# Sparse attention and a two-layer MLP on one core: weights loaded ahead of batch 1, each chunk's two layers in turn, one PSUM pool for both

## The chip, the core and the metric

One NeuronCore of one Trainium2 chip. The metric is the device time of one execution in microseconds (us); medians of several executions are given. An execution with a profile also leaves a trace; its "span" runs from the first to the last traced instruction and is about 1.8 us shorter than the time of the same execution (352.0 against 353.79 us for the kernel before).

## The reference

```python
q, k, v: (8, 8, 576, 64)  float32        # batch, heads, sequence, head size
scores = q @ k.T / sqrt(64)
heads 0-3: row sees the last 32 columns;  heads 4-7: row sees every 32nd column (causal)
attn   = softmax(masked scores) @ v
x      = attn as (8*576, 512) = (4608, 512)
h      = x @ w_in                         # (512, 2048)
out    = (max(h, 0) + alpha * min(h, 0)) @ w_out     # (2048, 512)
```

## The kernel before

TensorE (PE in the profile) does all matrix products in float16; here their outputs lie in the PSUM memory, all other tiles in the SBUF. The attention of a batch is cut into "pieces": S (scores), P (value blocks), T (transposes of queries and keys), X (transposes back into `xT`). The 4608 tokens go through the MLP in 9 chunks of 512; a layer of a chunk is 16 pieces of four 512-column matmuls. The pieces of both kinds are laid into each engine's program in the order in which Python calls them.

```python
pspool = tile_pool("ps", bufs=3, PSUM)      # transposes, value blocks
phpool = tile_pool("ph", bufs=2, PSUM)      # first layer
pbpool = tile_pool("pb", bufs=1, PSUM)      # scores, two banks
popool = tile_pool("po", bufs=1, PSUM)      # second layer
# ...
def over_v(b, eng):                          # 32 value rows repeated at other partitions
    v16 = vls[b % 2]
    cast_copy(eng, v16[0:32, 1:24, :], v16[96:128, 0:23, :])
# ... a score piece of a later batch ends on GpSimd:
    nc.scalar.activation(et, sp, Exp, scale=SCALE)
    nc.gpsimd.tensor_tensor(ev, ev, mask, op=mult)
# ... in the list of pieces, stage g (pair g's scores, pair g-1's value blocks):
    def run(...):
        if kind == "P0" and g % 4 == 1:
            over_v(g // 4, "dve")            # right ahead of the first value block
        fn()
        for b, pr in extra:                  # behind it, on GpSimd:
            cast_l(b, pr) ...                # casts of the next batch's q and k, or
            cast_v(b, pr, "pool") ...        # copies of the values
# ... one first-layer piece:
    hps = pspool.tile(...) if alone and m % 3 == 2 else phpool.tile(...)
    4 matmuls -> hps
    nc.scalar.activation(neg, hps, Relu, scale=-1.0)
    late.append(lambda: nc.vector.scalar_tensor_tensor(gT, neg, oma, hps, mult, add))
# ... order of the work behind batch 0 (cut):
for m in range(16): lin1_piece(0, m, True); attn_n(0 if m < 9 else 1, end1)
while pos["i"] < end1: attn_step(end1)       # rest of batch 1, alone
for m in range(16): lin1_piece(1, m, True); attn_n(0 if m < 13 else 1, end2)
for i in range(16): lin2_piece(0, i); attn_n(2 if i % 2 else 1, end2)
# ...
for n in range(2, NCH):                      # batch n+2 runs beside chunk n
    for i in range(16):
        lin2_piece(n, i);     attn_step(ab)
        lin1_piece(n + 1, i); attn_step(ab)
```

The softmax here doesn't subtract the row's maximum and nothing guards it: scores larger than these inputs give would overflow.

## Time and profile before

| | before |
|---|---|
| median time (first 3 runs) | 354.47 us |
| span of the profiled execution | 352.0 us |
| TensorE busy | 96% |
| DVE / ACT / POOL busy | 56% / 50% / 42% |
| granted clock at half | 50.7 to 60.9 us |

DVE is VectorE, ACT ScalarE, POOL GpSimd. The granted clock is what the profile records of TensorE's clock, as a share of full speed. A row of the timeline has the start, the length, engine and line, operation, output and inputs; a bracket has the idle time ahead of it and what ended that.

### The profile page before, as it was taken

What the parts mean: (1) busy time and instruction counts of PE and PEld (TensorE: products, weight loads), DVE (VectorE), ACT (ScalarE), POOL (GpSimd) and SP (SyncE); (2) the same over time, 40 slices, a digit from 0 to 9 for tenths busy, and PEclk for the clock granted to TensorE, in tenths of its full rate; (3) what the DMA queues carried; (4) which work ended last, traced back from release to release, by engine and by line L of the source; (5) the groups of instructions that cost most, each with busy time, mean ns of one, the idle gap of its engine ahead of it and who ended that gap; (6) DMA issues with size and microseconds to landing.
All of it is one profiled execution on the core that took longest, in us unless ns stands there. A gap on an engine that the chain in (4) does not pass through costs nothing.

```text
span 352.0 us, 6757 instructions
## 1 busy us (share of the span) xinstructions
PE 336.4 (96%) x2733; PEld 175.7 (50%) x2733; DVE 198.3 (56%) x391; ACT 176.6 (50%) x313; POOL 147.4 (42%) x164
## 2 busy tenths in 40 slices
PE   7899979999898998999999999999999999999995
PEld 2554544454444544554467665545455444444444
DVE  3487774884443875576557655765575444444400
ACT  2635852665336574656465646565645444444411
POOL 7936726259895583656365532451240000000000
PEclk9999985999999999999999999999999999999999
DMA  7999999934946862553556210000001100100021
GB/s 232 185 203 224 234 253 151 184 34 69 160 99 176 75 164 57 87 48 61 177 85 62 49 47 31 32 31 32 30 32 40 52 30 31 61 30 30 32 89 61
DMA packets 46111, 33.08 MB, mean 94 GB/s; under 512 B 27376, under 2 KB 37760, under 8 KB 46080
## 3 DMA queue, kind: packets, MB, share of 16 engines
q0 software_dynamic: 37312, 16.79, 44.6%
q1 hardware_dynamic: 8768, 15.87, 12.8%
q8 instruction: 21, 0.34, 0.4%
q14 instruction: 10, 0.08, 0.1%
HBM read 36.83 MB, written 9.44 MB: 131 GB/s over the span
## 4 chain that ended last, share of the span: by engine, by line
PE 86%; DVE 4%; POOL 4%; ACT 3%; DMA 1%; issue 1%; SPq 0%; ACTq 0%
PE hps L489 36%; PE ops L534 32%; PE sp L271 3%; PE tp L214 3%; PE pv L318 3%; DVE x L327 2%; PE xp L335 2%; POOL et L305 2%; DMA ql<-in_q_dram 1%; PE wps L556 1%; ACT kT L159 1%; PE sp L287 1%; PE ops L525 1%; ACT osb L539 1%; PE sph L287 1%
## 5 line engine op out<-in xcount | busy, mean ns | idle before, releaser
L502 DVE SCALAR_TENSOR_TENSOR gT<-neg,oma,hps 128x512 f16<-128x512 f32 x144 | 106.9, 743 | 74.7 <-ACT neg L499 72.4
L489 PE MATMUL hps<-xT,win 128*128 128x512 f16 (+1 forms) x640 | 146.7, 361 | 0.1
L534 PE MATMUL ops<-wout,gT 128*128 128x512 f16 x560 | 141.9, 379 | 1.9 <-ACT osb L539 1.6
L499 ACT ACTIVATE neg<-hps 128x512 f32<-128x512 f32 x144 | 86.2, 599 | 95.1 <-PE hps L489 93.6
L305 POOL TENSOR_TENSOR et<-et,consts 128x576 f16<-128x576 f16 (+1 forms) x48 | 61.3, 1277 | 80.5 <-ACT et L295 80.4
L489 PEld LDWEIGHTS <-win 128*128 128x128 f16 x640 | 58.4, 98 | 52.9 <-issue 3.4
L534 PEld LDWEIGHTS <-gT 128*128 128x128 f16 x560 | 49.7, 97 | 50.7 <-issue 2.5
L295 ACT ACTIVATE et<-sp 72x576 f16<-72x576 f32 (+1 forms) x58 | 37.6, 649 | 24.8 <-PE sp L271 11.7
L327 DVE TENSOR_TENSOR x<-pv,rc 72x384 f16<-72x384 f32 (+2 forms) x80 | 42.1, 527 | 2.7
L325 DVE RECIPROCAL rc<-pv 72x6 f32<-72x6 f32 (+2 forms) x80 | 14.9, 187 | 41.7 <-PE pv L318 41.4
L539 ACT COPY osb<-ops 128x512 f32<-128x512 f32 x35 | 20.6, 587 | 27.9 <-PE ops L534 27.9
L318 PEld LDWEIGHTS <-et 72*128 72x128 f16 (+1 forms) x448 | 23.2, 99 | 17.1 <-DVE x L327 1.8
L271 PEld LDWEIGHTS <-kT 64*128 64x128 f16 x448 | 10.9, 95 | 27.8 <-issue 17.7
L271 PE MATMUL sp<-qT,kT 64*128 64x72 f16 (+1 forms) x408 | 17.6, 201 | 3.5 <-ACT kT L159 3.2
L161 DVE COPY qT<-tp 128x1024 f16<-128x1024 f16 (+1 forms) x16 | 17.4, 1085 | 4.1 <-PE tp L214 4.1
L159 ACT COPY kT<-tp 128x1024 f16<-128x1024 f16 (+1 forms) x16 | 14.5, 909 | 6.7 <-PE tp L214 6.7
L556 PE MATMUL wps<-wrm 128*128 128x512 f16 x44 | 16.4, 448 | 1.2 <-DVE wrm L568 1.2
L318 PE MATMUL pv<-vs,et 72*128 72x65 f16 x256 | 15.4, 194 | 2.1 <-POOL et L305 0.8
L335 PEld LDWEIGHTS <-x 72*128 72x128 f16 (+1 forms) x224 | 12.4, 102 | 7.6 <-DVE x L327 2.4
L335 PE MATMUL xp<-consts,x 72*128 72x72 f16 (+1 forms) x224 | 14.7, 208 | 1.0 <-DVE x L327 0.8
L163 POOL COPY vs<-stv 72x1024 f16<-72x1024 f16 x14 | 14.5, 1061 | 0.0
L318 PE MATMUL pv<-vl,et 128*128 128x65 f16 x192 | 12.0, 200 | 1.2 <-DVE vl L161 1.1
(66 smaller groups left out, 189.6 us busy)
## 6 DMA issues: line engine op xcount, KB each, us to landing
out_dram<-osb SPq DMA_DIRECT2D x35, 256.0 KB, 2.0
ql<-in_q_dram SPq DMA_DIRECT2D x6, 512.0 KB, 5.2
kl<-in_k_dram SPq DMA_DIRECT2D x6, 512.0 KB, 5.9
stv<-in_v_dram POOLq DMA_DIRECT2D x8, 288.0 KB, 5.3
vl<-in_v_dram POOLq DMA_DIRECT2D x8, 288.0 KB, 8.3
win<-in_moe_w_in_dram POOLq DMA_DIRECT2D x4, 512.0 KB, 10.3
wout<-in_moe_w_out_dram POOLq DMA_DIRECT2D x4, 512.0 KB, 16.8
qs<-in_q_dram POOLq DMA_DIRECT2D x7, 256.0 KB, 4.6
```

The source lines that it names most:

```text
L271: keep(nc.tensor.matmul(sps[y][:, w * x : w * x + w], P.kT[hf, k0 : k0 + 128], P.qT[hf, w * t : w * t + w], start=(x == 0), stop=(x == len ...
L295: keep(nc.scalar.activation(ev.rearrange("r (y c) -> r y c", y=2), sp[0:r, :, 0:n], AF.Exp, scale=SCALE))
L305: keep(nc.gpsimd.tensor_tensor(ev, ev, m, op=ALU.mult))
L318: keep(nc.tensor.matmul(pv[:, 65 * x : 65 * x + 65], et[0:r, c : c + 128], v16[0:r, 2 * P.pr + hh, t, :] if P.strided else v16[:, 6 * (2 * ...
L327: keep(nc.vector.tensor_tensor(P.x16[0:w, c0 : c0 + 64 * nb].rearrange("r (c e) -> r c e", e=64), pvv[:, :, 0:64], rc[0:w, 0:nb].unsqueeze ...
L335: keep(nc.tensor.transpose(xp[:, P.w * t : P.w * t + P.w], P.x16[0 : P.w, 128 * t : 128 * t + 128], ident[0 : P.w, 0 : P.w]))
L489: keep(nc.tensor.matmul(hps[:, dst : dst + w], win16[:, kk, 128 * m : 128 * m + 128], xT[:, kk, src : src + w], start=(kk == 0 and x == 0) ...
L499: keep(nc.scalar.activation(neg, hps, AF.Relu, scale=-1.0))
L502: keep(nc.vector.scalar_tensor_tensor(gTs[n][:, m, :], neg, oma[:, m : m + 1], hps, op0=ALU.mult, op1=ALU.add))
L534: keep(nc.tensor.matmul(ops, gTs[n][:, kf, 128 * mt : 128 * mt + 128], wout16[:, kf, :], start=(kf == 0), stop=(kf == 15)))
L539: keep(nc.scalar.copy(osb, ops))
L556: keep(nc.tensor.matmul(wps, wrm[:, 0:128], wrm, start=True, stop=True))
```

## The change

Its intent: nothing of batch 1 is to delay the weights, chunk 0 is to run through both layers while batch 1 comes in, no stretch of attention is to stand alone, and a freed PSUM bank is to serve whichever layer runs.

```diff
-    phpool = tile_pool(name="ph", bufs=2, PSUM)
+    phpool = tile_pool(name="ph", bufs=3, PSUM)
-    popool = tile_pool(name="po", bufs=1, PSUM)      # lin2 and warm-up now take phpool too
@@ loads ahead of batch 1
     load_w(2, False)
-    load_unit(1, True, False)
+    load_w(3, False)
...
-    load_w(3, False)
-    load_v(1, True)
+    for c in range(4): load_w(c, True)
+    load_unit(1, True)
     load_unit(1, False)
@@ order
     for m in range(16):
-        lin1_piece(0, m, True)
-        attn_n(0 if m < 9 else 1, end1)
+        lin1_piece(0, m)
+        attn_n(0, end1)
+    for i in range(16):
+        lin2_piece(0, i)
+        attn_n(0 if i < 6 else 2, end1)
     while pos["i"] < end1: attn_step(end1)
-    (lin1 of chunk 1, lin2 of 0, half of lin2 of 1, lin1 of 2 with the rest ...)
-    for n in range(2, NCH): (lin2 of n and lin1 of n+1 by turns, batch n+2 beside)
+    for n in range(1, NCH):                   # batch n+1 beside chunk n
+        left = ab - pos["i"];  skip = 4 if n == 1 else 0;  acc = 0.0
+        for i in range(32):
+            lin1_piece(n, i) if i < 16 else lin2_piece(n, i - 16)
+            if i >= skip:
+                acc += left / (23.5 - 0.5 * skip) * (0.5 if i < 16 else 1.0)
+            cnt = int(acc); acc -= cnt
+            attn_n(cnt, ab)
```

Within batch 1 some pieces also change places (the transposes of the second unit come behind the value blocks of the first), and some loads and casts of batches 1 and 2 move; both are cut here.

More of the change, by code (lines that the diff above doesn't have):

```diff
@@ L63 @@
     pspool = ctx.enter_context(tc.tile_pool(name="ps", bufs=3, space=bass.MemoryType.PSUM))
-    phpool = ctx.enter_context(tc.tile_pool(name="ph", bufs=2, space=bass.MemoryType.PSUM))
+    phpool = ctx.enter_context(tc.tile_pool(name="ph", bufs=3, space=bass.MemoryType.PSUM))
     pbpool = ctx.enter_context(tc.tile_pool(name="pb", bufs=1, space=bass.MemoryType.PSUM))
-    popool = ctx.enter_context(tc.tile_pool(name="po", bufs=1, space=bass.MemoryType.PSUM))
     keep(nc.scalar.add_instruction(
@@ L362, in X, with alone @@
         return lambda: x_piece(pairs[g])
-    def alone(u0, u1):
+    def alone(u0, u1, ahead):
         A, L = (2 * u0, 2 * u0 + 1), (2 * u1, 2 * u1 + 1)
@@ L371, in alone @@
                 feed(Sc(g, i), -1)
-        feed(T(u1, "q"), -1)
-        feed(T(u1, "k"), -1)
-        for i in range(2):
-            feed(Sc(L[0], i), -1)
+        if ahead:
+            feed(T(u1, "q"), -1)
+            feed(T(u1, "k"), -1)
+            for i in range(2):
+                feed(Sc(L[0], i), -1)
         for g in A:
@@ L378, in alone @@
                 feed(Pv(g, i), -1)
+        if not ahead:
+            feed(T(u1, "q"), -1)
+            feed(X(A[0]), -1)
+            feed(T(u1, "k"), -1)
+            feed(X(A[1]), -1)
+            for i in range(2):
+                feed(Sc(L[0], i), -1)
         for i in range(2):
             feed(Sc(L[1], i), -1)
-        for g in A:
-            feed(X(g), -1)
+        if ahead:
+            for g in A:
+                feed(X(g), -1)
         for g in L:
@@ L390, in alone @@
             feed(X(g), -1)
-    alone(1, 0)
+    alone(1, 0, True)
     end0 = len(pieces)
-    alone(3, 2)
+    alone(3, 2, False)
     end1 = len(pieces)
@@ L474, with lin1_piece @@
     gTs = {}
-    def lin1_piece(n, m, alone=False):
+    def lin1_piece(n, m):
         if m == 0:
@@ L482, in lin1_piece @@
             parts.append((0, RING - c0, 512 - (RING - c0)))
-        if alone and m % 3 == 2:
-            hps = pspool.tile([128, 512], F32, tag="ps", name="hps3")
-        else:
-            hps = phpool.tile([128, 512], F32, tag="hps", name="hps")
+        hps = phpool.tile([128, 512], F32, tag="hps", name="hps")
         for kk in range(4):
@@ L511, in lin2_piece @@
         if part == 0:
-            if last and mt % 2 == 1:
-                ops_cur["t"] = phpool.tile([128, 512], F32, tag="hps", name="ops2")
-            else:
-                ops_cur["t"] = popool.tile([128, 512], F32, tag="ops", name="ops")
+            ops_cur["t"] = phpool.tile([128, 512], F32, tag="hps", name="ops")
         ops = ops_cur["t"]
@@ L559 @@
     wrm = cpool.tile([128, 512], F16)
-    wps = popool.tile([128, 512], F32, tag="ops", name="wps")
+    wps = phpool.tile([128, 512], F32, tag="hps", name="wps")
     def load_unit(b, strided, v_too=True):
@@ L596 @@
     keep(nc.gpsimd.memset(vss[1][:, :, :, 64:65], 1.0))
-    load_w(3, False)
-    load_v(1, True)
+    for c in range(4):
+        load_w(c, True)
+    load_unit(1, True)
     load_unit(1, False)
@@ L626, in attn_n @@
             attn_step(0)
-    wide["on"] = False
-    for c in range(4):
-        load_w(c, True)
-    cast_l(1, "q")
-    cast_l(1, "k")
+    load_qk(2, False, "q")
+    load_qk(2, False, "k")
     for pr in range(2):
         cast_v(1, pr, "pool")
-    load_unit(2, False)
+    cast_l(1, "q")
+    load_tail(2, False)
+    cast_l(1, "k")
+    load_v(2, False)
     load_unit(2, True)
+    cast_l(2, "q")
+    cast_l(2, "k")
     for m in range(16):
-        lin1_piece(0, m, True)
-        attn_n(0 if m < 9 else 1, end1)
-    wide["on"] = True
+        lin1_piece(0, m)
[3 more added lines that the diff above has]
+        attn_n(0 if i < 6 else 2, end1)
     while pos["i"] < end1:
@@ L644 @@
     wide["on"] = False
-    cast_l(2, "q")
-    cast_l(2, "k")
     load_unit(3, False)
     load_unit(3, True, False)
-    end2 = attn_until(2)
-    for m in range(16):
-        lin1_piece(1, m, True)
-        attn_n(0 if m < 13 else 1, end2)
-    for i in range(16):
-        lin2_piece(0, i)
-        attn_n(2 if i % 2 else 1, end2)
-    for i in range(8):
-        lin2_piece(1, i)
-        attn_n(1, end2)
-    while pos["i"] < end2:
-        attn_step(end2)
-    end3 = attn_until(3)
-    for m in range(16):
-        lin1_piece(2, m)
-        attn_n(1, end3)
-        if m % 2:
-            lin2_piece(1, 8 + m // 2)
-            attn_n(2, end3)
-    while pos["i"] < end3:
-        attn_step(end3)
-    for n in range(2, NCH):
-        ab = attn_until(n + 2) if n + 2 < B else len(pieces)
-        for i in range(16):
-            lin2_piece(n, i)
-            attn_step(ab)
-            if n + 1 < NCH:
-                lin1_piece(n + 1, i)
-                attn_step(ab)
+    for n in range(1, NCH):
+        ab = attn_until(n + 1) if n + 1 < B else len(pieces)
+        left = ab - pos["i"]
+        skip = 4 if n == 1 else 0
+        acc = 0.0
+        for i in range(32):
+            if i < 16:
+                lin1_piece(n, i)
+            else:
+                lin2_piece(n, i - 16)
+            if i >= skip:
+                acc += left / (23.5 - 0.5 * skip) * (0.5 if i < 16 else 1.0)
+            cnt = int(acc)
+            acc -= cnt
+            attn_n(cnt, ab)
         while pos["i"] < ab:
```

## The prediction

> **What bounds the kernel now.** I read the page first (busy shares, clock row, chain), then the table by stage, then TensorE's own waits, then the timeline of its one slow stretch. The chain and the busy shares say TensorE:
>
> ```profile
> PE 336.4 (96%) x2733; PEld 175.7 (50%) x2733; DVE 198.3 (56%) x391; ACT 176.6 (50%) x313; POOL 147.4 (42%) x164
> ...
> PEclk9999985999999999999999999999999999999999
> ...
> PE 86%; DVE 4%; POOL 4%; ACT 3%; DMA 1%; issue 1%; SPq 0%; ACTq 0%
> ```
>
> But 96% busy does not tell how much is avoidable, because ends of matmuls are modelled. So I count streaming time instead. In the pure second-layer stretch of the timeline,
>
> ```profile
> 333.95 10.52 PE L534 MATMUL ops<-wout,gT 128*128 128x512 f16 x48
> ```
>
> 48 matmuls start within 10.36 us (the next group starts at 344.31), 0.216 us each; a "piece" of either layer (4 of them) is 0.863 us, a layer of a 512-token chunk (16 pieces) 13.8 us. All layer work from the first piece (26.58) to TensorE's end (348) is 1072 full matmuls and 160 half ones, 249.0 us. The rest of those 321.4 us, 72.4 us, is attention of batches 1 to 7 plus everything lost. The table by stage splits it:
>
> ```profile
> 26.58:57.06 30.48, 27.40 (x260) 15.47 (x259) 22.56 (x46) 18.20 (x35) 15.79 (x20) 0.90 1.75 222
> 57.06:140.33 83.27, 78.23 (x667) 39.47 (x667) 50.99 (x95) 43.22 (x75) 56.80 (x60) 0.98 0.82 115
> 140.33:261.00 120.67, 120.56 (x1119) 67.40 (x1119) 75.50 (x150) 68.53 (x120) 55.77 (x52) 1.00 0.31 60
> ```
>
> (first number the length; then busy us of PE, weight load, DVE, ACT, POOL; then granted clock.) From 140 to 261 us nothing waits: 369 full and 128 half layer matmuls are 93.4 us, the remaining 27.2 us are 3.46 batches of attention (194 value matmuls of 56 a batch), **7.9 us a batch**. Batch 1 adds 16 mask matmuls of about 0.125 us, so about 9.8. Batches 1 to 7 at these rates need 9.8 + 6 x 7.9 = 57.2 us, so **about 15 us of the 72.4 are lost**, all before 140 us. By stage: 30.5 - 14.0 (65 layer matmuls) - 9.8 = 6.7 us up to 57.06; 83.3 - 55.9 (259 layer matmuls) - 2.3 batches x 7.9 (18.1) = 9.3 us up to 140. Two causes show in the first part of that:
>
> ```profile
> 45.21 0.28 PE L242 MATMUL tt<-consts,tl 128*128 128x128 f16 x2
> 46.82 0.30 PE L271 MATMUL sp<-qT,kT 64*128 64x96 f16 x6 [1.33 <-ACT kT L159]
> ...
> 49.20 0.34 PE L318 MATMUL pv<-vs,et 72*128 72x65 f16 x6 [0.66 <-DVE rc L325]
> 49.80 0.36 PE L318 MATMUL pv<-vs,et 72*128 72x65 f16 x6 [0.26 <-DVE x L327]
> ```
>
> ```profile
> 47.28:50.70 3.42, 2.32 (x48) 1.69 (x46) 2.49 (x9) 1.26 (x3) 1.38 (x2) 1.00 1.26 289
> 50.70:57.06 6.36, 5.83 (x69) 4.04 (x66) 5.06 (x15) 2.49 (x5) 1.76 (x3) 0.50 2.38 162
> 57.06:60.94 3.88, 3.86 (x10) 1.24 (x9) 1.20 (x2) 0.63 (x2) 3.88 (x6) 0.50 1.19 162
> ```
>
> Batch 1's last 19 attention pieces run with no layer work between, so TensorE waits for ScalarE and VectorE; and right after that thin stretch the clock is granted at half for 10.24 us (50.70 to 60.94), also under the next chunk's first layer.
>
> [...]
>
> **The change part by part.**
>
> 1. *Weights first.* The fourth first-layer piece and all of the second layer's weights are issued ahead of batch 1. Before, the first-layer weights are issued 10.0 to 16.6 and land from 18.0 to 29.7; the second layer's 28.3 to 32.9, landing from 41.3 to 51.4. [...]After: by 29.7 us all of the first and about one quarter of the second have come (the batch-1 loads between them now follow); three more at the 3.9 us of the slowest reading ((29.7 - 18.0)/3) end by about 41.4. Chunk 0's second layer starts at 26.6 + 13.8 = 40.4 and needs its last quarter 2.6 us later, at 43. No stall. Batch 1's loads follow at about 1.3 us each for the strided ones, in time for its first transpose near 46.5.
> 2. *Batch 1 spread over chunk 0's second layer.* 20 of its 26 pieces lie two by two behind 10 layer pieces; its last 6 (four value blocks, two transposes back) still run alone. Removed: the 6.7 us, and the half clock under the next layer (3.88/2 = 1.9 us). New: the 6 alone. VectorE needs four times reciprocal and multiply (0.19 + 0.55) and two copies of 0.45, 3.9 us with a hop, against 1.25 us of TensorE's own work there: **about 3.0 us lost** before the next first layer may start.
> 3. *That stretch and the clock.* It streams for about 0.3 of 4 us. [...]Expected, **1.5 us**.
> 4. *Batches 2 and 3.* The rest of the loss, 9.3 - 1.9 = 7.4 us, goes with the old order (three pieces per two layer pieces from 74 us on, one PSUM buffer for second-layer outputs, 1.6 us of waits for its copy). After, batch 2 still comes 33 pieces in 28 slots: I keep **1.7 us** for it (one 0.7 us wait for the transposed keys, one for the mask on GpSimd such as the 0.84 us seen at 88).
> 5. *New wait at each chunk border.* Batch n+1 now ends exactly where chunk n+1's first layer wants it; before, it was a chunk ahead. The built order shows on TensorE, for chunks 1 to 6: last second-layer piece, last transpose back, first first-layer piece. That transpose is copied by ScalarE (0.64 us) behind the output copy (0.59 us), both started 0.2 us after TensorE, so it is ready at 1.51; TensorE has 0.28 (transposes) + 3 x 0.216 = 0.93 us before the quarter that needs it. 0.58 us lost, six times: **3.4 us**.
> 6. *First layer in one run.* Every 0.863 us a VectorE step of 0.743 and a ScalarE one of 0.599, plus 8 attention pieces: VectorE 16 x 0.743 + 3 x 0.74 + 0.45 + 0.44 = 15.0 us against TensorE's 13.8 + 2.4 = 16.2. Walking one such run by hand with three buffers, one wait of 0.2 us comes out: **1 us** over five chunks. The old first layer with three buffers ran at 0.863 us a piece, so three are enough when it is alone.
>
> Sum on the traced span: 352.0 - 15 (losses removed, 6.7 + 9.3 rounded down since 7.9 holds small stalls) + 3.0 + 1.5 + 1.7 + 3.4 + 1.0 + 0.5 (small) = 348.1 us. The timed runs are 2.5 us longer than the trace's span (354.47 to 352.0): **350.5 us**.
>
> **Rivals.** (a) *Clean gain*: the copy at the border hides better and the clock stays full: minus 4 to 5 us, 346. For it: ScalarE is only half busy. Against: [...]the copy stands behind the output's. (b) *VectorE becomes the bound* in the first-layer runs: it is 92% busy there by my count, and each wait for a buffer repeats; one us a chunk more gives 356. Against: the first layer alone ran without waits at 86% (0.743/0.863). (c) *Transfers*: batch 1 or the weights arrive late, chunk 0 stalls by some us and the clock drops: 354 to 357. For it: the DMA engines are full up to 60 us. Against: 1.6 us of slack or more on the slow reading. (d) *Nothing*: the new waits equal the old losses, 354.
>
> **Range and chances.** Around 350.5 the clock is worth +-2, the border and VectorE waits +-2 each, the old loss estimate +-1.5: 346 to 355. Over 2% faster means under 347.4: 0.24. Within 2%: 0.73. Over 2% slower, above 361.6: 0.03.
>
> **What would show each step.** Right: chunk 0's second layer starts near 40.4 us and has no wait for weights; one thin stretch near 62 to 67 us, with a half-clock record behind it[...] shorter than 10.24 us; six waits of 0.5 to 0.7 us of first-layer matmuls for ScalarE's transpose copy; waits of first-layer matmuls for VectorE summing to about 1 us; TensorE's end about 4 us earlier. Wrong: waits for weights or queries before 50 us, first-layer waits for VectorE of several us, a full 10 us at half clock, or borders without waits.

The sum came to 348.1 us on the span and 350.5 us of time. Of part 3 the 1.5 us stands in the sum as an estimate of mine, to which the traces give no derivation. What they do show is the case of before: 10.24 us at half clock behind a thin stretch. The full DMA engines of rival (c) are the DMA row of the page, 90% or more from 8.8 to 70 us; in part 1 the 1.3 us of a strided load of 256 KB fits its GB/s row, 185 to 253 from 8.8 to 53 us (1.0 to 1.4 us).

## More of the kernel before

The prediction reads the page and the stages line by line. One group that it passed over is the copy of `over_v`, here in the view of the tile `vl` (shortest, median and longest ns, first and last start):

```profile
L161 DVE COPY vl<-vl x8: 542/543/1494, 21.9 to 237.5; 32x1495 f16<-32x1495 f16 x8
```

The same instruction on the same shape, eight times: 0.54 us in six of them, but 1.49 for batch 2 and 0.92 for batch 3.

## The result

The changed kernel took 358.73 us (median of 4; 357.81 to 359.31) against 354.14 us: the ratio is 1.0126 (95% interval 1.0096 to 1.0155), so 1.3% slower. A ratio is the mean time of one kernel's fast runs over that of the other's in the same rounds, so it is not quite the ratio of the quoted medians. This lies outside the stated range and on the other side of 1. Executions over 1.5% slower than the fastest of the same kernel are left out of the means.

The page of the changed kernel, lines of busy shares, of the clock (40 slices) and of the chain:

```profile
PE 335.5 (94%) x2733; PEld 174.7 (49%) x2733; DVE 207.5 (58%) x391; ACT 175.5 (49%) x315; POOL 146.6 (41%) x164
PEclk9999999996999799999999999999999999999999
PE 85%; DVE 7%; ACT 3%; DMA 2%; issue 1%; SPq 0%; ACTq 0%
```

The half clock of before is gone from its place (slices 6 and 7), but two new ones stand at slices 10 and 14, VectorE's share of the chain has risen from 4% to 7%, and VectorE is 9 us busier with the same instructions. The stages, cut at the first layer of chunk 1 and of chunk 2 (columns as in the prediction):

```profile
26.73:67.57 40.84, 38.55 (x323) 19.82 (x322) 22.99 (x47) 20.42 (x41) 20.64 (x26) 1.00 1.50 192
67.57:119.65 52.08, 42.35 (x356) 21.78 (x356) 35.65 (x51) 21.95 (x39) 31.42 (x34) 0.88 0.71 116
119.65:300.00 180.35, 178.63 (x1559) 95.75 (x1557) 111.13 (x215) 98.78 (x174) 76.86 (x73) 1.00 0.33 64
```

By the prediction's own rates, chunk 0 (128 layer matmuls, 27.6 us, and batch 1, 9.8) has 3.4 us of loss, where 3.0 had been expected. Chunk 1 (27.6 us, and 33 attention pieces at 7.9/26 each, 10.0) has **14.4 us** of loss. The rest runs with hardly a gap. TensorE's waits name the cause, and the timelines around 80 us, of TensorE, VectorE and GpSimd in this order, show it:

```profile
PE pv L317 <- DVE vl L160: 9.4, 2, 5.5
PE hps L494 <- ACT xT L338: 1.6, 5, 0.3
```

```profile
80.56 0.19 PE L317 MATMUL pv<-vl,et 128*128 128x65 f16 x1
86.27 0.44 PE L317 MATMUL pv<-vl,et 128*128 128x65 f16 x5 [5.51 <-DVE vl L160]
```

```profile
80.87 5.34 DVE L160 COPY vl<-vl 32x1495 f16<-32x1495 f16 x1
```

```profile
80.77 1.03 POOL L162 COPY vs<-stv 72x1024 f16<-72x1024 f16 x1
81.75 0.80 POOL L143 DMA_DIRECT2D stv<-in_v_dram  x1
82.56 1.29 POOL L304 TENSOR_TENSOR et<-et,consts 128x576 f16<-128x576 f16 x1
83.78 1.05 POOL L162 CAST ql<-ql 128x1024 f16<-128x1024 f32 x1
84.77 1.03 POOL L162 CAST kl<-kl 128x1024 f16<-128x1024 f32 x1
```

The copy of 0.54 us starts 0.1 us after GpSimd has begun an instruction, and ends at 86.21: 0.41 us after GpSimd's last one of an unbroken run (84.77 + 1.03 = 85.80). For batch 3 the same at 111.67: 4.65 us long, 0.41 us behind the end of GpSimd's run. The tile view of `vl`, as above but in the changed kernel:

```profile
L160 DVE COPY vl<-vl x8: 543/1354/5344, 22.1 to 260.1; 32x1495 f16<-32x1495 f16 x8
```

So batches 2 and 3 are not alone: those of batches 4, 5 and 6 took 1.37, 1.36 and 1.35 us in the timeline, each ending 0.42 us behind the one GpSimd instruction that it had met, without a wait in TensorE's list. In the kernel before, batch 2's copy and GpSimd at that time:

```profile
75.70 1.49 DVE L161 COPY vl<-vl 32x1495 f16<-32x1495 f16 x1
```

```profile
75.51 1.28 POOL L305 TENSOR_TENSOR et<-et,consts 128x576 f16<-128x576 f16 x1 [0.66 <-ACT et L295]
76.74 1.36 POOL L163 COPY vs<-stv 72x1024 f16<-72x1024 f16 x1
```

There it slipped in behind one GpSimd instruction (it ended at 77.19, 0.40 us after 76.79), although the next began without a gap, and the next GpSimd copy took 1.36 us in place of 1.03. The conflict was there all along; the old order met it in a harmless form.

The second part of the cost, after the waits (columns as above; the clock is the third number from the end):

```profile
80.24:83.65 3.41, 0.51 (x4) 0.20 (x2) 3.38 (x2) 0.96 (x2) 3.39 (x4) 1.00 0.09 5
83.65:90.48 6.83, 4.21 (x19) 2.01 (x19) 4.71 (x5) 0.93 (x2) 2.15 (x3) 0.50 0.26 41
110.96:114.37 3.41, 1.54 (x13) 0.66 (x12) 3.35 (x4) 0.65 (x1) 3.39 (x4) 1.00 0.95 243
114.37:121.20 6.83, 4.83 (x29) 2.77 (x29) 3.92 (x4) 1.13 (x2) 1.54 (x2) 0.50 0.38 98
```

In the 3.41 us ahead of each of the two stretches TensorE was busy for 0.51 and 1.54 us; the granted clock was then 0.50 for 6.83 us, twice. At half clock four 512-column matmuls took 1.91 us (from 117.45 us), at full clock 1.04 (from 111.43). TensorE was busy for 4.21 and 4.83 us of the two stretches, of which about half was lost: 4.5 us. Waits 9.4 + clock 4.5 = 13.9 of the 14.4 us.

**Theory.** This copy on VectorE, of 16-bit data within the SBUF, does not get through as long as GpSimd runs without a gap: 5.34 and 4.65 us, each ending 0.41 us behind GpSimd's run (the copy of the kernel before, which took 1.49 us and ended 0.40 us behind one instruction of a longer run, does not fit this). What keeps it out, the traces do not show. **Rivals.** The copy waited for its data or its place in a queue; VectorE as such was late; the half clock costs nothing beyond the wait.

### The profile page after: what moved, and what is told of

The parts are those of the page before. It is cut to its first block, busy times and chain, and to the rows that moved or that the text cites. A ratio compares the mean times of both kernels' runs of the same rounds, so it can differ in the third digit from the quotient of the medians.

```text
span 357.3 us, 6745 instructions
## 1 busy us (share of the span) xinstructions
PE 335.5 (94%) x2733; PEld 174.7 (49%) x2733; DVE 207.5 (58%) x391; ACT 175.5 (49%) x315; POOL 146.6 (41%) x164
## 3 DMA queue, kind: packets, MB, share of 16 engines
q1 hardware_dynamic: 8768, 15.87, 12.7%
## 4 chain that ended last, share of the span: by engine, by line
PE 85%; DVE 7%; ACT 3%; DMA 2%; issue 1%; SPq 0%; ACTq 0%
PE hps L494 35%; PE ops L536 32%; PE sp L270 4%; PE pv L317 4%; PE tp L213 3%; DVE vl L160 3%; DVE x L326 3%; PE xp L334 2%; DMA kl<-in_k_dram 2%; PE wps L558 1%; PE ops L527 1%; ACT xT L338 1%; PE sph L286 1%; PE sp L286 1%; ACT osb L541 1%
## 5 line engine op out<-in xcount | busy, mean ns | idle before, releaser
L494 PE MATMUL hps<-xT,win 128*128 128x512 f16 (+1 forms) x640 | 137.5, 363 | 2.0 <-ACT xT L338 1.6
L536 PE MATMUL ops<-wout,gT 128*128 128x512 f16 x560 | 138.8, 381 | 0.0
L494 PEld LDWEIGHTS <-win 128*128 128x128 f16 x640 | 59.4, 99 | 57.6 <-issue 6.9
L536 PEld LDWEIGHTS <-gT 128*128 128x128 f16 x560 | 48.6, 98 | 45.3 <-issue 0.6
L294 ACT ACTIVATE et<-sp 72x576 f16<-72x576 f32 (+1 forms) x56 | 36.2, 647 | 19.6 <-PE sp L270 13.2
L160 DVE COPY vl<-vl 32x1495 f16<-32x1495 f16 x8 | 15.7, 1962 | 0.2
```

Source lines behind the costliest of these rows:

```text
L160: keep(nc.vector.tensor_copy(o, i))
L294: keep(nc.scalar.activation(ev.rearrange("r (y c) -> r y c", y=2), sp[0:r, :, 0:n], AF.Exp, scale=SCALE))
L494: keep(nc.tensor.matmul(hps[:, dst : dst + w], win16[:, kk, 128 * m : 128 * m + 128], xT[:, kk, src : src + w], start=(kk == 0 and x == 0) ...
L536: keep(nc.tensor.matmul(ops, gTs[n][:, kf, 128 * mt : 128 * mt + 128], wout16[:, kf, :], start=(kf == 0), stop=(kf == 15)))
```

## The experiments

Twelve kernels were run, and all gave correct results. Diffs are against the changed kernel unless said otherwise; "run 5" is the kernel of section 5. Ratios are to the kernel before in the same rounds. Four executions of each are quoted (the profiled one and three timed), one for run 12.

### 1. The copy on ScalarE, same place

```diff
-                    over_v(g // 4, "dve")
+                    over_v(g // 4, "act")
```

> Theory[...]: in the changed kernel VectorE's 32x1495 copy of the value rows (0.54 us when free) sat 5.34 us for batch 2 and 4.65 us for batch 3, each time until a back-to-back run of GpSimd instructions ended, and TensorE waited 9.4 us for it, after which the clock was halved twice. ScalarE does the same copy here for batches 2 to 7. [...]no wait of TensorE for this copy over 1.5 us, no half-clock record around 84 and 114 us, time about 346 us, ratio to before about 0.978. Rival (the copy waited for its data, or the value blocks would be late anyway through the denser order): TensorE still waits several us at the first value block of batches 2 and 3, and the ratio stays near 1.01.

Measured: 355.87 us, ratio 1.0049 (1.0015 to 1.0083). No copy was stretched any more, but all six stood in TensorE's way, so the time missed the forecast by 10 us:

```profile
PE pv L317 <- ACT vl L158: 7.7, 6, 2.1
```

Each took 1.42 to 1.43 us on ScalarE, and the one of batch 3 started only at 108.18 us, behind the exponential that TensorE's previous piece had fed (0.65 us from 107.64). So this run neither confirms nor refutes the theory by its time: I had not counted that the copy stands directly ahead of its reader. The longest wait did fall from 5.5 to 2.1 us, more than the 1.5 forecast, and the clock was not full throughout: its mean was 0.994 in the profiled execution (0.980 in the changed kernel's).

### 2. The copy on VectorE, same place, as a reduction

```diff
+        if eng == "red":
+            keep(nc.vector.tensor_reduce(<32 x 1495>, <32 x 1495 x 1>, axis=X, op=max)); return
-                    over_v(g // 4, "dve")
+                    over_v(g // 4, "red")
```

> Same engine and same place as in the changed kernel, but as a maximum over one element[...]. Theory:[...] TensorE waits about 1 us for each; no half clock at 84 and 114 us; time 347 to 351 us, ratio 0.98 to 0.99. Rival (VectorE as such is late, or GpSimd blocks any VectorE instruction): durations of 4 to 6 us for batches 2 and 3 again, ratio about 1.01.

Measured: 351.53 us, ratio 0.9930 (0.9910 to 0.9951). The forecast of the duration was that the reduction takes the same time in all six batches. The tile view (shortest, median, longest ns):

```profile
L176 DVE TENSOR_REDUCE vl<-vl x6: 1700/1701/1701, 82.3 to 252.1; 32x1495 f16<-32x1495 f16 x6
```

Three times slower than the free copy and never longer than 1.70 us, though GpSimd was as busy as before (at 82.3 us it ran a copy, a DMA issue and a mask without a gap). Same engine, same place, same data, same readers: this rules out the rivals about data, queue or VectorE as such. What is left is something that holds up this copy and not this reduction while GpSimd runs; what that is, no trace shows. The durations are steady: 1.70 us as a reduction here and 1.42 to 1.43 us on ScalarE in run 1, in all six batches. TensorE still waited 4.2 us in six waits, and the mean clock was 0.995 where the changed kernel's was 0.980: by an estimate from these means (twice what is missing to 1, times the span) about 3.5 us at half in place of 14; the time is just above the 347 to 351 us expected.

### 3. Less GpSimd work behind the copy

```diff
+        if g % 4 == 1:
+            nslots = nslots[-2:]      # the next batch's two casts come later
```

> Dose: only the two GpSimd casts (2.05 us together) that follow the copy in the program are moved behind the later value block and the key transpose. Theory (copy blocked for as long as GpSimd runs without a gap, then 0.41 us): copies of about 3.0 to 3.4 us for batch 2 and 2.7 us for batch 3 in place of 5.34 and 4.65, TensorE's waits for them down from 9.4 to about 5 us, time 350 to 355 us. Rival (blocked for one GpSimd instruction only, or by something else): durations unchanged or down to about 1.4 us.

Measured: copies of 3.40 and 2.70 us, as expected to the tenth. VectorE, then GpSimd:

```profile
83.17 3.40 DVE L160 COPY vl<-vl 32x1495 f16<-32x1495 f16 x1
```

```profile
83.07 1.03 POOL L162 COPY vs<-stv 72x1024 f16<-72x1024 f16 x1
84.05 0.80 POOL L143 DMA_DIRECT2D stv<-in_v_dram  x1
84.86 1.29 POOL L304 TENSOR_TENSOR et<-et,consts 128x576 f16<-128x576 f16 x1
```

GpSimd's run ends at 86.15, the copy at 86.57, 0.42 us behind it. TensorE's waits for it fell to 5.5 us. The time fell into two groups: 356.13 to 356.38 us in three executions at granted clocks of 0.980 to 0.986 (one of the three is marked slow, for it is 1.5% above the fourth), and 351.02 us in one at 0.999. So its ratio, 1.0011 (0.9933 to 1.009), says little; only the one execution lies in the 350 to 355 us expected. The two groups lie 5 us apart, and the fast executions alone already show it: at mean clocks of 0.980 and 0.986 356.13 and 356.19 us, at 0.999 351.02.

### 4. The wait kept, TensorE kept busy

```diff
                     over_v(g // 4, "dve")
+                    if g // 4 in (2, 3):
+                        wf = phpool.tile([128, 512], F32, tag="hps", name="wf")
+                        for _ in range(18): matmul(wf, wrm[:, 0:128], wrm)     # result unused
```

> The stalls stay, but 18 dummy matmuls of 512 columns (3.9 us) lie on TensorE ahead of the first value block of batches 2 and 3[...]. Theory (the halved clock is caused by the stalls and costs time by itself): copies as long as before, no half-clock record before the end, time about 4.5 us less than the changed kernel, near 354 us, ratio about 1.00. Rival (the clock costs nothing beyond the wait): ratio 1.01 as the changed kernel, or more by the dummies.

Measured: 355.14 us, ratio 1.0044 (1.0013 to 1.0076). The copy of batch 2 came as late as before: from the start of the dummies to the value matmuls that need it 5.71 us passed (80.25 to 85.96), in the changed kernel 5.71 from the first value matmul (80.56 to 86.27). In the profiled execution the mean clock was 1.000. One execution had a lower mean clock (0.994) and took 356.56 us; the other three, at 0.998 to 1.000, took 354.89 to 355.15, some 3.6 us under the changed kernel's median where 4.5 had been expected. So the half clock is a cost of its own. The count of 4.5 us was made on the profiled execution of the changed kernel, which took 359.04 us; against the profiled one here (354.89 us) the difference is 4.15.

### 5. The copy early, on ScalarE

```diff
-                if kind == "P0" and g % 4 == 1:
-                    over_v(g // 4, "dve")
+                if kind == "S" and firsts and g % 4 == 0:      # first piece of the batch
+                    over_v(g // 4, "act")
```

> The copy of the value rows on ScalarE as before, but issued one pair (7 pieces or so) ahead of the value block that needs it, so that neither GpSimd nor the queue of ScalarE stands between. Theory: no wait of TensorE for it at all, half clock at most one window behind batch 1's thin stretch near 67 us; the changed kernel's 358.7 us less 9.4 us of waits less 3 to 4.5 us of clock = 345 to 347 us, ratio 0.974 to 0.981. Rival (the waits only move to the keys, the masks or the border): ratio above 0.985.

Measured: **346.08 us, ratio 0.9762 (0.9736 to 0.9788)**. No wait for the copy is left in TensorE's list. The profiled execution (346.88 us, mean clock 0.993) ran at half clock behind batch 1's thin stretch: its first four first-layer matmuls, from 67.55 us, took 2.05 us, where four at full clock took 1.03 (from 104.47). Another with the same mean clock took 346.53 us, and two at 1.000 and 0.998 took 345.57 and 345.62: 1.1 us less. Chunk 1 now takes 40.74 us (67.55 to 108.29), where the changed kernel took 52.08. So the rest of the change was worth 2.4%, and the one copy took it all away and 1.3% more: 12.7 us by the medians, from waits and clock together.

### 6. The copy early, on VectorE

```diff
+                if kind == "S" and firsts and g % 4 == 0:
+                    over_v(g // 4, "dve")
```

> The copy stays on VectorE[...], only earlier by one pair. Tells whether engine or place matters. Theory: the copy is still stretched where GpSimd runs without gaps (some of 1.4 to 3 us), but TensorE does not wait for it directly; it delays VectorE's queue instead, so the first-layer steps or the value blocks wait a little: 346 to 349 us. Rival[...]: 353 us or more.

Measured: 346.12 us, ratio 0.9770 (0.9750 to 0.9791).

```profile
L160 DVE COPY vl<-vl x8: 543/544/698, 22.0 to 241.8; 32x1495 f16<-32x1495 f16 x8
```

The time is as in 5, but by a better reason than I had: at this place GpSimd pauses (for batch 2 0.76 us, up to 78.92 us, for the batch's first exponential), so the copy is hardly stretched, longest 0.70 us. Between these two engines the choice does not matter here (346.12 against 346.08 us); the place does. What a stretched copy would do at an early place stays untried.

### 7. The same in the kernel before

> The kernel before with the same early copy on ScalarE. In its trace the copy took 1.49 us for batch 2, 0.92 for batch 3 and 0.54 for the rest, and TensorE waited for it once, 1.07 us. Theory[...]: 0 to 1.5 us less, ratio 0.996 to 1.0. Rival (the gain of the early copy is general and has nothing to do with the new order): 3 us or more, ratio under 0.992.

The edit of 5 in the kernel before. Measured: 353.93 us, ratio 1.0005 (0.9990 to 1.0020): no gain, at the low edge of what was expected. The early copy is no general improvement. But this run does not show the cost of the conflict alone. TensorE's wait of 1.07 us for the copy is gone, and that was for batch 4's, a copy of 0.54 us in the trace of before. In its place TensorE's list has a wait of 1.5 us for an exponential of ScalarE, which now does the copy too.

### 8. Batch 1 earlier

```diff
# on top of 5
-        attn_n(0 if i < 6 else 2, end1)
+        attn_n(0 if i < 3 else 2, end1)
```

> The run before, and batch 1 begins behind piece 3 of chunk 0's second layer in place of piece 6, so that its last six pieces no longer stand alone. Theory: the thin stretch near 63 to 67 us and its 3.0 us of loss go but for about 0.5 us, and with it the half-clock window that some executions had near 67 us: 2.5 to 4 us less than the run before. Rival (batch 1's data come too late, TensorE waits for transfers or casts between 44 and 55 us): no gain or a loss.

Measured: 343.90 us, ratio 0.9705 (0.9686 to 0.9723), 2.2 us under run 5, a little less than the 2.5 to 4 us expected. The last value blocks and transposes now lie between second-layer pieces, the clock is 0.999 or more in all four executions, and no wait for a transfer appears.

### 9. The border between chunks

```diff
# on top of 5
-                acc += left / (23.5 - 0.5 * skip) * ...
+                acc += left / (22.5 - 0.5 * skip) * ...
```

> As the first of these runs, but each batch's pieces are spread a little tighter, so that one second-layer piece follows the last transpose back of chunks 1 to 6. Theory: the six waits of the first layer for ScalarE's copy (2.0 us in the list of waits, about 0.5 us each on TensorE) go: 2 to 3 us less than the first of these runs. Rival (the border is hidden already and the list overstates it): within 1 us.

The border between chunks, first in run 5, then here (transpose back, then layer pieces):

```profile
143.89 0.42 PE L334 MATMUL xp<-consts,x 72*128 72x72 f16 x8
144.15 0.81 PE L494 MATMUL hps<-xT,win 128*128 128x512 f16 x3
145.31 1.24 PE L494 MATMUL hps<-xT,win 128*128 128x512 f16 x5 [0.35 <-ACT xT L338]
```

```profile
142.93 0.42 PE L334 MATMUL xp<-consts,x 72*128 72x72 f16 x8
143.19 1.03 PE L536 MATMUL ops<-wout,gT 128*128 128x512 f16 x4
144.06 1.89 PE L494 MATMUL hps<-xT,win 128*128 128x512 f16 x8
```

In the first, the fourth matmul starts 1.16 us after the group of three, which needs 0.65: 0.51 us late. In the second nothing waits. Yet the time was 345.67 us, ratio 0.9756, 0.4 us under run 5: as to the time, the rival held. Part of the gain was given back in chunk 1, where the tighter spread made TensorE wait longer for keys and exponentials (2.4 and 1.4 us in its list in place of 1.4 and 0.7).

### 10. Runs 5, 8 and 9 together

> All three together: if they add up, 5 to 7 us less than the first of these runs, 339 to 342 us, ratio to before 0.957 to 0.968. If the waits hide one another, less.

Measured: 343.17 us, ratio 0.9685 (0.9666 to 0.9704): the gains add up only to 2.9 us under run 5, less than expected.

### 11. The tighter spread from chunk 2 on only

```diff
# on top of 8
+                acc += left / ((23.5 if n == 1 else 22.5) - 0.5 * skip) * ...
```

> The run with all three changes, but the tighter spread only from chunk 2 on: in chunk 1, where 33 pieces lie, it had cost 1.5 us by waits for keys and exponentials (excess of 70 to 90 us). Theory: those come back and the border stays mended: 341 to 342.5 us, ratio 0.963 to 0.967. Rival (the border wait only moves): 343 us or more as before.

Measured: **342.23 us, ratio 0.9672 (0.9658 to 0.9687)**, as expected and the fastest, 3.3% under the kernel before. Its page, busy shares and clock:

```profile
PE 330.2 (97%) x2733; PEld 173.1 (51%) x2733; DVE 193.5 (57%) x385; ACT 182.9 (54%) x321; POOL 146.3 (43%) x164
PEclk9999999999999999999999999999999999999999
```

Against run 8 the mended borders are worth 1.2 us by the ratios, where five times 0.51 would be 2.6. By the first first-layer matmul of each chunk, chunks 3 to 7 are 0.36, 0.26, 0.36, 0.31 and 0.51 us shorter than in run 8 and chunk 2 is 0.14 longer, 1.7 us in all; so within most chunks part of the gain is lost again, to what was not followed up.

### 12. Two PSUM pools in the new order

```diff
# on top of 5
-    phpool bufs=3        (first layer, second layer)
+    phpool bufs=2        (first layer);  popool bufs=1 (second layer)
```

> The first early-copy run with the PSUM pools as the kernel before had them (two buffers for the first layer, one for the second). A buffer is held for 0.86 (matmuls) + 0.2 + 0.60 (ScalarE) + 0.74 (VectorE) + 0.1 = 2.5 us; with two, a piece of an unbroken first-layer run takes 1.25 us in place of 0.86, 6 us more for a run without attention and about 4 us more for one with: 380 to 395 us. Rival (the third buffer is not needed): within 5 us of 346.

401.7 us. TensorE's waits, and the first layer of chunk 0:

```profile
PE hps L495 <- DVE gT L508: 23.7, 49, 1.0
PE ops L537 <- ACT osb L542: 12.1, 23, 0.7
```

```profile
29.35 1.89 PE L495 MATMUL hps<-xT,win 128*128 128x512 f16 x8 [0.61 <-DVE gT L508]
31.84 1.89 PE L495 MATMUL hps<-xT,win 128*128 128x512 f16 x8 [0.60 <-DVE gT L508]
```

Two pieces every 2.49 us, 1.25 us each as worked out ahead; the second layer's waits for its one buffer had been left out of the forecast. So the pool is not a refinement: the new order cannot do with the old split. It is one execution in an unknown state, but the 55 us are far outside any spread seen here.

## Why the prediction was wrong, point by point

The time on record was 350.5 us in a range of 346 to 355; it was 358.7. The step that failed is **4, "Batches 2 and 3"**, and in it the term "I keep 1.7 us for it". Chunk 1 lost 14.4 us: 9.4 in two waits for the copy of the value rows, 4.5 by the clock that the waits brought down (runs 2, 3, 5 and 6 show the first part, run 4 and the split of run 3 the second). None of the four rivals named it, and even the worst of them ended at 357. The sign was in the trace of before: one instruction on one shape, 0.54 us six times but 1.49 and 0.92 us for batches 2 and 3, a group mean of 708 ns. I took the mean for its price and asked for no reason for the spread. I had named only TensorE's waits, and in their list the two stretched copies did not show at all: the one wait for this tile, 1.07 us at 132 us, was for batch 4's copy of 0.54 us. In run 5, with the copy out of the way, chunk 1 loses 40.74 - 37.6 = 3.1 us, time at half clock included, against the forecast 1.7 plus 1.5 for the clock. That this fits is partly luck: the waits named for it (keys 0.7, mask 0.84 us) are not those found (keys 0.2, exponentials 0.7 us).

- **1, weights first**: right. Chunk 0's second layer started at 40.81 us (forecast 40.4) with no wait for weights. Not tried alone; what it contributes by itself stays open.
- **2, batch 1 spread**: right; 3.4 us of loss in the stage against 3.0.
- **3, the clock there**: in the profiled execution nothing happened: the granted clock was 1.00 from 66.59 to 70.00 us, though TensorE was busy for 2.32 us of the 3.41 us ahead (63.18 to 66.59), as much as in the stretch of before that half clock had followed (2.32 of 3.42 us, 47.28 to 50.70). The 3.41 us ahead of that one were thinner, 2.08 us (43.87 to 47.28), and the clock behind them stayed at 1.00. So the busy time alone does not decide, and what does was not shown. In run 5 half clock did follow the stretch (from 67.55 us, above). Two of its four executions had the lower mean clock (0.993), and it cost them 1.1 us: 1.5 us expected, about a third of that found on average. The lengths measured in the two traces, 6.83, 6.83 and 10.24 us, are two, two and three times 3.41 us.
- **5, the border**: mechanism and size of one wait right (0.58 forecast, 0.51 found), but mending it paid 1.2 us by the ratios and 1.7 by the traces (run 11), not 3.
- **6, first layer in one run**: right; TensorE's list has no first-layer wait for VectorE, so even the 1 us was too much. Run 12 shows what three buffers are for.
- **The sum**: with the copy out of the way the change stands at 346.1 us, 4.4 below the sum. The offset from span to time was 0.7 too large, since I set the span of one execution (which took 353.79 us) against the median of several; the clock, the first-layer waits and the small reserve make up about 2.5; the remaining 1.2 us were not traced.

Open: what keeps the copy out, and why it got in between two GpSimd instructions at 76.8 us in the kernel before, and not in the longer runs.

## What to carry to other kernels

When a schedule is made denser, look for instructions whose duration varies on one shape, before asking what the change adds: the spread (here 0.54 to 1.49 us) can be a conflict that depends on when they run, and it need not show in any wait yet. The 32x1495 16-bit copy within the SBUF on VectorE that TensorE needed at once took 5.34 and 4.65 us where GpSimd had a backlog; issued a few pieces ahead, where GpSimd paused, the same instruction took 0.54 to 0.70 us (run 6). And a long wait of TensorE can cost more than its length: behind waits of 5.5 and 3.9 us the clock was halved, for 4.5 us more.
